# An expert's chunks past the third, moved from the end of the stage into the third chunk's condition

## The chip, the cores and the metric

The kernel runs on one core of a Trainium2 chip. Five engines work at once, each through its own list of instructions: TensorE (PE in the profile, PEld for its weight loads), VectorE (DVE), ScalarE (ACT), GpSimd (POOL) and SyncE (SP, which only starts transfers here). Rows with a small q behind the engine (PEldq, POOLq) are what its sequencer does: branches, semaphores, transfers that it issues. The metric is the device time of one launch in microseconds (us), lower is better.

## What is computed

Three parts in a row, on 1152 tokens of 512 numbers; the second and third matter here. Cut to what counts (`lg` are the logits of a token over eight experts):

```python
x = attention(q, k, v)                       # (1152, 512)
# part 2: each token goes to its best expert; an expert takes the first `capacity` of its tokens
e = argmax(x @ w_gate);  p = softmax value of e
out[i] = p[i] * (relu(x[i] @ w1[e]) @ w2[e]) if kept else 0        # capacity is 288
# part 3: tokens with x @ w_skip > 0 go through experts of their own, without a capacity
x[i] += p[i] * (relu(x[i] @ v1[e]) @ v2[e])
```

So how many tokens an expert gets is known only when the kernel runs: up to 288 in part 2, and in part 3 up to 1152.

## The kernel before

**Staging.** Attention ends at about 350 us. Then `experts(m, ...)` runs twice, for part 2 (m = 0, about 350 to 510 us) and for part 3 (m = 1, about 560 us to the end), with the routing of part 3 between them. The rows of an expert's tokens lie together in a scratch tensor `xs` in device memory, and an expert's rows are worked on in chunks of 128. Weights are loaded once per expert (`raw`), split into a high and a low part by ACT and DVE (`hi`, `lo`), while PE works on the expert before.

**One expert.** The first chunk of every expert is computed without a condition (`block_t`, whose matmuls are at L937, L947 and L957). Then comes a condition for the second chunk (L1172, more than 128 tokens), in it a choice between a whole and a half chunk (L1173), and in it the condition for the third chunk (L1178, more than 256) with its own choice (L1179). The tokens of chunk 2 and 3 are read from `xs` by `load_x` (L901). An expert's result goes to the output by an indirect transfer that POOL issues in `put` (L885).

**What is past the third chunk.** NPRE is 3, so three chunks are 384 tokens. For an expert with more, `rest` (from L1105) runs a loop, one more chunk for each turn. It stands at the end of the stage: a condition at L1188 on the largest of the eight counts (computed with the counts, L324), and in it, for each of the eight experts, a loop of at most one turn that loads and splits its weights again (`reload`) and calls `rest`.

**What follows a stage.** Behind m = 0, five loads by SP (L1215) read the output back for part 3. They wait for all the puts. PE goes on at once with the first chunk of the eighth expert (`last_block`), into which the transposes `gx` (L258) of the rows read back are mixed. Behind m = 1 the kernel ends.

**Conditions.** Each engine has its own copy of each condition: it reads the count, compares and branches. All code of a condition's body lies in the engine's list between the branch and the join. An engine that doesn't enter runs a short block in its place that brings the semaphores to the values which the body would have left; PE's block first waits for PE's own semaphore, that is until its matmuls so far are done. Rows of the trace with EVENT_SEMAPHORE or INC_SWDGE_SEM at a condition's line are that block, so they are there only where it was not entered. The order of the code is the order of the program, there is no scheduler.

Of the kernel before, what the change touches and what calls it, by code (L numbers as in the profile page):

```python
# [8 lines left out]
F32 = mybir.dt.float32  # L9
F32R = mybir.dt.float32r  # L10
BF16 = mybir.dt.bfloat16
I32 = mybir.dt.int32
AF = mybir.ActivationFunctionType
ALU = mybir.AluOpType
AX = mybir.AxisListType

P = 128
# [4 lines left out]
def fused_kernel(  # L22
# [15 lines left out]
    nc = tc.nc  # L38
    B, H, S, D = q.shape
    SQ = S // 2  # L40
    N, DM = out.shape
    E = wg1.shape[1]
    F = w1a.shape[2]
    KD = DM // P
    KF = F // P
# [6 lines left out]
    ROW = DM + 8  # L52
    REG = N
    NPRE = 3
# [4 lines left out]
    keep = ctx.enter_context(tc.tile_pool(name="keep", bufs=1))  # L59
# [86 lines left out]

    slot_i = keep.tile([P, NT], I32, name="slot_i")
    cnt = [keep.tile([P, E], F32, name=f"cnt{m}") for m in range(2)]
    cnt_i = [keep.tile([1, E + 1], I32, name=f"cnt_i{m}") for m in range(2)]
    mask = [keep.tile([P, E, NPRE], F32, name=f"mask{m}") for m in range(2)]  # L150

    def masks(m):
# [160 lines left out]
    def count(ps_r, ohs, limit, m):  # L313

        t = ps_r()[:, 0:E]
        mms = [o[:, j, :] for o, n_o in ohs for j in range(n_o)]
        for n, o in enumerate(mms):
            nc.tensor.matmul(t, ones, o, start=(n == 0), stop=(n == len(mms) - 1))
        if limit is not None:
            nc.vector.tensor_scalar(cnt[m], t, limit, None, op0=ALU.min)  # L320
        else:
            nc.vector.tensor_copy(cnt[m], t)
        nc.vector.tensor_copy(cnt_i[m][:, 0:E], cnt[m][0:1, :])
        nc.vector.tensor_reduce(out=cnt_i[m][:, E : E + 1], in_=cnt_i[m][:, 0:E], axis=AX.X, op=ALU.max)  # L324

    def warm(ps, n):

# [68 lines left out]
    with ExitStack() as actx:  # L396
# [328 lines left out]
        def flush(x, n):  # L725
            for _ in range(min(n, len(x))):
                x.pop(0)()

        ex = []
        for idx in range(len(items) + LAG):  # L730
# [6 lines left out]
            if cur and at in (0, NFC):  # L737
                flush(preps, len(preps))
                m = cur[0] + 1 + (at > 0)
# [14 lines left out]
            if cur:  # L754
                n, c = cur
                if at in (NFC - 1, 2 * NFC):
                    flush(preps, len(preps))
                m = n + (2 if at < NFC else 3)
# [9 lines left out]
            if old:  # L768
                n, c = old
# [16 lines left out]
        wp = [wctx.enter_context(tc.tile_pool(name="wp0", bufs=2, **kw))]  # L786
        w_t = {}
# [63 lines left out]
    with ExitStack() as mctx:  # L851
# [67 lines left out]
        def new_xx(name):  # L919
            return xo.tile([P, 2, KD, P], F32R, tag="xx", name=name)  # L920
# [165 lines left out]
                )  # L1086
            put(m, yt, dropped, x, HP)

        def reload(m, e):

            for half in range(2):
                hi, lo = w_t[m, e, half] = tuple(
                    wp[0].tile([P, KD * F], F32R, tag=t, name=f"{t}r{m}_{e}_{half}") for t in ("hi", "lo")
                )
                kk = (KD, KF)[half]
                src = ((w1a, w2a), (w1b, w2b))[m][half][e].rearrange("(c p) f -> p c f", p=P)
                for r in range(4):
                    raw = hp.tile([P, F], F32, tag="hs", name="raw")
                    c = slice(r * kk // 4, (r + 1) * kk // 4)
                    s = slice(r * F, (r + 1) * F)  # L1100
                    nc.sync.dma_start(out=raw.rearrange("p (c f) -> p c f", c=kk // 4), in_=src[:, c, :])
                    nc.scalar.copy(hi[:, s], raw)
                    nc.vector.tensor_tensor(out=lo[:, s], in0=raw, in1=hi[:, s].bitcast(F32), op=ALU.subtract)

        def rest(m, e, n_e, xx):  # L1105

            iv = sm.tile([P, 1], F32, tag="iv", name="iv")
            nc.vector.tensor_scalar_add(iv, rowid[:, 0:1], float(NPRE * P))

            pad = sm.tile([P, 1], F32, tag="pad", name="pad")  # L1110
            nc.vector.tensor_tensor(out=pad, in0=cnt[m][:, e : e + 1], in1=rowid[:, 0:1], op=ALU.add)
            big = sm.tile([P, 1], F32, tag="big", name="big")
            nc.vector.tensor_scalar(big, pad, float(REG), BIG, op0=ALU.is_ge, op1=ALU.mult)
            pi = sm.tile([P, 1], I32, tag="pi", name="pi")
            nc.vector.scalar_tensor_tensor(out=pi, in0=pad, scalar=float(e * REG), in1=big, op0=ALU.add, op1=ALU.add)
            z = xb.tile([P, ROW], F32, tag="x2", name="z", bufs=1)
            nc.vector.memset(z, 0.0)
            nc.gpsimd.indirect_dma_start(
                out=xs,
                out_offset=bass.IndirectOffsetOnAxis(ap=pi, axis=0),  # L1120
                in_=z,
                in_offset=None,
                bounds_check=E * REG - 1,
                oob_is_err=False,
            )
            with tc.For_i(NPRE * P, n_e, P) as i:
                lt = sm.tile([P, 1], F32, tag="lt", name="lt")
                nc.vector.tensor_tensor(out=lt, in0=cnt[m][:, e : e + 1], in1=iv, op=ALU.is_le)
                x = xb.tile([P, ROW], F32, tag="x2", name="xr", bufs=1)
                nc.sync.dma_start(out=x, in_=xs[bass.ds(i + e * REG, P), :])  # L1130
                xprep(x, xx)
                block_t(m, e, x, xx, lt, [], [], c_tile, d_tile)
                nc.vector.tensor_scalar_add(iv, iv, float(P))

        def experts(m, first, count_all, loads=()):


            x, xx = load_x(m, 0, 0), new_xx("xx0")
            two_parts(first, xx)
            count_all()  # L1140
            masks(m)
            x_n = load_x(m, 1, 0)
            x_1 = load_x(m, 0, 1)
            flush(loads, len(loads))
            for e in range(E):
                late = []
                steps = split_ops(m, e + 1, late) if e + 1 < E else []
                preps = []
                x_nn = load_x(m, e + 2, 0) if e + 2 < E else None
                none = [mask[m][:, e, c : c + 1] for c in range(NPRE)]  # L1150
                if e + 1 < E:
                    x_1n = load_x(m, e + 1, 1)
                if m == 0 and e == E - 1:
                    xx_1, xx = xx, new_xx("xx0")
                    xprep(x, xx)
                else:
                    if m == 0 and e == E - 2:
                        xx_1, xx_n = new_xx("xx1"), new_xx("xxn")
                        preps += [lambda: xprep(x_1, xx_1), lambda: xprep(x_1n, xx_n)]
                    else:  # L1160
                        if e + 1 < E:
                            xx_n = new_xx("xxn")
                            preps.append(lambda: xprep(x_n, xx_n))
                        xx_1 = new_xx("xx1")
                        preps.append(lambda: xprep(x_1, xx_1))
                    block_t(m, e, x, xx, none[0], steps, preps, a_tile, b_tile)
                if e == 0:
                    _, vals = nc.values_load_multi_w_load_instructions(cnt_i[m][0:1, :], min_val=0, max_val=N)
                n_e = vals[e]
                x_2 = xb.tile([P, ROW], F32, tag="x2", name=f"x{m}_{e}_2", bufs=1)  # L1170
                xx_2 = new_xx("xx2")
                with tc.If(n_e > P):  # L1172
                    with tc.If(n_e > P + HP) as more:  # L1173
                        load_x(m, e, 2, x_2)
                        block_t(m, e, x_1, xx_1, none[1], [], [lambda: xprep(x_2, xx_2)], c_tile, d_tile)
                    with more.Else():
                        block_h(m, e, x_1, xx_1, none[1], [], [], c_tile, d_tile)
                    with tc.If(n_e > 2 * P):  # L1178
                        with tc.If(n_e > 2 * P + HP) as more:  # L1179
                            block_t(m, e, x_2, xx_2, none[2], [], [], d_tile, c_tile)  # L1180
                        with more.Else():
                            block_h(m, e, x_2, xx_2, none[2], [], [], d_tile, c_tile)
                flush(late, len(late))
                if e + 1 < E:
                    x, xx, x_1, x_n = x_n, xx_n, x_1n, x_nn
            kept = [w_t[m, E - 1, half] for half in range(2)]

            with tc.If(vals[E] > NPRE * P):  # L1188
                xxr = new_xx("xxr")
                for e in range(E):  # L1190
                    with tc.For_i(NPRE * P, vals[e], N):
                        reload(m, e)
                        rest(m, e, vals[e], xxr)
            w_t[m, E - 1, 0], w_t[m, E - 1, 1] = kept
            return x, lambda fill, yt: block_t(m, E - 1, x, xx, none[0], fill, [], a_tile, b_tile, yt)

        x_last, last_block = experts(0, first, lambda: count(lambda: b_tile([P, 512], "pc0"), ohs, cap[:, 0:1], 0))
# [15 lines left out]
        for c, n in ((0, 1), (1, 2), (3, 2), (5, 2), (7, 2)):  # L1213
            src = out[c * P : (c + n) * P, :].rearrange("(c p) d -> p c d", p=P)
# [123 lines left out]
```

## Time and profile before

| | us |
|---|---|
| median of three runs | 720.62 (719.03 to 723.29) |
| the profiled execution, its own time | 716.99 |
| its span, from the first instruction to the last | 715.1 |

| engine | busy us | share of the span |
|---|---|---|
| PE | 660.8 | 92% |
| PEld | 487.7 | 68% |
| DVE | 446.7 | 62% |
| ACT | 436.1 | 61% |
| POOL | 128.4 | 18% |

PE is busy nearly all the time, so time is lost where PE stands still: each gap on PE is read with what ended it. The granted TensorE clock has a mean of 0.982 of full speed over the execution. An engine's instructions reach it by transfers of their own, the queues q8 (PE) and q14 (the others).

### The profile page before, as it was taken

What the parts mean: (1) busy time and instruction counts of PE and PEld (TensorE: products, weight loads), DVE (VectorE), ACT (ScalarE), POOL (GpSimd) and SP (SyncE); (2) the same over time, 40 slices, a digit from 0 to 9 for tenths busy, and PEclk for the clock granted to TensorE, in tenths of its full rate; (3) what the DMA queues carried; (4) which work ended last, traced back from release to release, by engine and by line L of the source; (5) the groups of instructions that cost most, each with busy time, mean ns of one, the idle gap of its engine ahead of it and who ended that gap; (6) DMA issues with size and microseconds to landing.
All of it is one profiled execution on the core that took longest, in us unless ns stands there. A gap on an engine that the chain in (4) does not pass through costs nothing. (4 is left out here: it accounts for less than half of the span.)

```text
span 715.1 us, 11137 instructions
## 1 busy us (share of the span) xinstructions
PE 660.8 (92%) x3978; PEld 487.7 (68%) x3978; DVE 446.7 (62%) x822; ACT 436.1 (61%) x961; POOL 128.4 (18%) x147
## 2 busy tenths in 40 slices
PE   7899999999999999998888999999779889999994
PEld 6766666666776666655766867776558677777773
DVE  5755656665655755556698638942176788998221
ACT  5876767676756757672687638832170768886210
POOL 4322222222221331002201011010035110001010
PEclk9999999999999999999999999999997999999998
DMA  6142624050200314014799917960444798994000
GB/s 175 41 142 107 218 107 171 17 188 31 82 17 2 114 38 152 1 19 176 263 334 339 337 46 266 329 222 18 147 137 156 247 348 314 369 339 149 27 30 13
DMA packets 55598, 111.38 MB, mean 156 GB/s; under 512 B 5470, under 2 KB 14686, under 8 KB 55488
## 3 DMA queue, kind: packets, MB, share of 16 engines
q1 hardware_dynamic: 52128, 102.27, 41.6%
q0 software_dynamic: 3360, 7.72, 2.8%
q8 instruction: 59, 0.97, 0.6%
q14 instruction: 51, 0.42, 0.2%
HBM read 93.51 MB, written 19.71 MB: 158 GB/s over the span
## 5 line engine op out<-in xcount | busy, mean ns | idle before, releaser
L807 DVE TENSOR_TENSOR lo<-raw,hi 128x512 fp32r<-128x512 f32 x248 | 155.6, 684 | 6.3 <-ACT hi L817 3.8
L817 ACT CAST hi<-raw 128x512 fp32r<-128x512 f32 x256 | 143.0, 623 | 8.4 <-PEq L1172 4.0
L527 PE MATMUL s_ps<-kop,qop 128*128 128x384 f32 x480 | 125.2, 369 | 2.2 <-ACT a L571 1.9
L601 PE MATMUL pt<-ident,a 128*128 128x128 f32 x648 | 109.7, 283 | 3.3 <-ACT kop L476 1.1
L555 DVE TENSOR_REDUCE m<-s_ps 128x1 f32<-128x1152 f32 x72 | 97.6, 1356 | 24.2 <-PE s_ps L527 21.5
L571 ACT ACTIVATE a<-s_ps,m 128x384 f32<-128x384 f32 (+1 forms) x144 | 106.8, 747 | 3.3 <-DVE m L555 3.2
L476 ACT COPY at<-pt 128x384 f32<-128x384 f32 x144 | 68.2, 481 | 64.1 <-PE pt L601 64.0
L601 PEld LDWEIGHTS pt<-ident,a 128*128 128x128 f32 x648 | 71.5, 140 | 46.1 <-ACT at L476 13.0
L627 PE MATMUL pv<-at,vr 128*64 128x320 f32 (+1 forms) x576 | 97.9, 428 | 0.0
L476 DVE COPY at<-pt 128x384 f32<-128x384 f32 x72 | 39.8, 552 | 76.3 <-PE pt L601 74.1
L527 PEld LDWEIGHTS s_ps<-kop,qop 128*128 128x128 f32 x480 | 74.6, 186 | 5.9 <-ACT a L571 4.3
L885 POOL DMA_INDIRECT out_dram<-yt,ix x23 | 24.9, 1084 | 285.7 <-DVEq L1172 149.1
L937 PE MATMUL ph<-hi,xxn 128*128 128x512 f32 x224 | 61.5, 406 | 13.2 <-PEq L1172 8.0
L950 DVE TENSOR_TENSOR hl<-pg,hh 128x512 fp32r<-128x512 f32 x42 | 29.0, 689 | 67.5 <-ACT hh L949 67.3
L941 ACT ACTIVATE hs<-ph 128x512 f32<-128x512 f32 x42 | 25.1, 598 | 60.3 <-PE ph L937 40.2
L937 PEld LDWEIGHTS ph<-hi,xxn 128*128 128x128 f32 x224 | 41.8, 192 | 26.9 <-ACTq L1172 7.0
L957 PE MATMUL py<-lo,hh 128*128 128x512 f32 x168 | 52.5, 414 | 0.0
L957 PE MATMUL py<-hi,hh 128*128 128x512 f32 x168 | 46.7, 399 | 1.3 <-ACT hh L949 0.8
L466 POOL TENSOR_TENSOR qhl<-qr,qhl 96x384 fp32r<-96x384 f32 x30 | 29.9, 1014 | 95.7 <-DVE qhl L464 95.7
L627 PEld LDWEIGHTS pv<-at,vr 128*64 128x64 f32 x576 | 30.0, 135 | 23.8 <-issue 18.3
L957 PE MATMUL py<-hi,hl 128*128 128x512 f32 x168 | 46.0, 395 | 0.0
L949 ACT CAST hh<-pg 128x512 fp32r<-128x512 f32 x42 | 24.6, 587 | 29.6 <-PE pg L947 27.7
(170 smaller groups left out, 891.8 us busy)
## 6 DMA issues: line engine op xcount, KB each, us to landing
raw<-in_moe_w_dram SPq DMA_DIRECT2D x64, 1024.0 KB, 7.3
x<-xs SPq DMA_DIRECT2D x36, 260.0 KB, 6.4
xs<-xtok SPq DMA_DIRECT2D x8, 780.0 KB, 7.4
qr<-in_q_dram SPq DMA_DIRECT2D x16, 288.0 KB, 3.4
vr<-in_v_dram SPq DMA_DIRECT2D x8, 576.0 KB, 6.1
kr_None<-in_k_dram SPq DMA_DIRECT2D x7, 576.0 KB, 5.0
out_dram<-xtok SPq DMA_DIRECT2D x3, 768.0 KB, 7.7
x<-out_dram SPq DMA_DIRECT2D x4, 512.0 KB, 5.7
```

Source lines behind the costliest of these rows:

```text
L466: sub.tensor_tensor(out=t[:, 1, :, r, :], in0=qs, in1=t[:, 0, :, r, :].bitcast(F32), op=ALU.subtract)
L476: (nc.vector.tensor_copy if on_vector else nc.scalar.copy)(dst, src)
L527: i = nc.tensor.matmul(s_ps[0:M, bank[j], 0 : 3 * P], qop[n + r][:, part, o : o + M], kop[n + r][:, j, :], start=(part == 0 and r == (c == ...
L555: i = nc.vector.tensor_reduce(out=nm, in_=s_ps[:, lo : lo + 3, 0 : 3 * P], axis=AX.XY, op=ALU.max, negate=True)
L571: i = nc.scalar.activation(a[:, a0 : a0 + nb, :], s_ps[:, b0 : b0 + nb, 0 : 3 * P], AF.Exp, bias=nm, accum_out=t[:, c, n % 2, k : k + 1],)
L601: nc.tensor.transpose(ps[:, x * P : (x + 1) * P], a[:, g, x * P : (x + 1) * P], ident)
L627: nc.tensor.matmul(hold["pv"][j * D : (j + 1) * D, 0:w], vrt[i][:, j, c * D : (c + 1) * D], at_t[2 * i + j, part][:, c, :], start=(c == 0) ...
L807: eng.tensor_tensor(out=lo, in0=raw, in1=hi.bitcast(F32), op=ALU.subtract)
L817: nc.scalar.copy(hi, raw)
L937: lambda d=d, i=i, a=a, b=b: nc.tensor.matmul(ps, xx[:, a, d, :], w1[b][:, d, s], start=(d + i == 0), stop=(d == KD - 1 and i == 2))
L950: nc.vector.tensor_tensor(out=hl[:, fs, :], in0=ps, in1=hh[:, fs, :].bitcast(F32), op=ALU.subtract)
L957: lambda f=f, i=i, a=a, b=b: nc.tensor.matmul(py, a[:, f, :], w2[b][:, f, :], start=(f + i == 0), stop=(f == KF - 1 and i == 2))
```

## The change

`rest` is called with its expert: in the third chunk's condition, behind the third chunk, there is one more condition, for more than 384 tokens, and `rest` in it, which takes the weights that are still there. The condition at the end of the stage goes away, with the reloading, the eight loops and the maximum of the counts. `rest` uses the tiles of the third chunk, `x_2` and `xx_2`, for the zero rows and the rows of a turn. Lines of the changed kernel: L1172 is L1153 there, L1178 is L1159, L937 is L936, L957 is L956, L1215 is L1189, and the new condition is L1164, with `rest`'s loop at L1108.

```diff
-    cnt_i = [keep.tile([1, E + 1], I32, name=f"cnt_i{m}") for m in range(2)]
+    cnt_i = [keep.tile([1, E], I32, name=f"cnt_i{m}") for m in range(2)]
...
-        nc.vector.tensor_copy(cnt_i[m][:, 0:E], cnt[m][0:1, :])
-        nc.vector.tensor_reduce(out=cnt_i[m][:, E : E + 1], in_=cnt_i[m][:, 0:E], axis=AX.X, op=ALU.max)
+        nc.vector.tensor_copy(cnt_i[m], cnt[m][0:1, :])
...
-        def reload(m, e):
...
-        def rest(m, e, n_e, xx):
+        def rest(m, e, n_e, x, xx):
...
-            z = xb.tile([P, ROW], F32, tag="x2", name="z", bufs=1)
-            nc.vector.memset(z, 0.0)
+            nc.vector.memset(x, 0.0)
...
             with tc.For_i(NPRE * P, n_e, P) as i:
...
-                x = xb.tile([P, ROW], F32, tag="x2", name="xr", bufs=1)
                 nc.sync.dma_start(out=x, in_=xs[bass.ds(i + e * REG, P), :])
...
                             block_h(m, e, x_2, xx_2, none[2], [], [], d_tile, c_tile)
+                        with tc.If(n_e > NPRE * P):
+                            rest(m, e, n_e, x_2, xx_2)
                 flush(late, len(late))
...
-            kept = [w_t[m, E - 1, half] for half in range(2)]
-
-            with tc.If(vals[E] > NPRE * P):
-                xxr = new_xx("xxr")
-                for e in range(E):
-                    with tc.For_i(NPRE * P, vals[e], N):
-                        reload(m, e)
-                        rest(m, e, vals[e], xxr)
-            w_t[m, E - 1, 0], w_t[m, E - 1, 1] = kept
```

The order of the instructions changes in the same way for each of the sixteen experts. On PE before, at the end of the first expert, the last matmuls of the half third chunk, the joins of the conditions (the unconditional branches; where one waits for PE, that is the block for not entering), and the second expert's first chunk:

```order
L1012 MATMUL py<-hi_0_1_3537,hx 128x512 x3
L1012 MATMUL py<-lo_0_1_3538,hx 64x512 x4
L1179 UNCONDITIONAL_BRANCH
L1178 UNCONDITIONAL_BRANCH [waits PE_49]
L1172 UNCONDITIONAL_BRANCH [waits PE_49]
L937 MATMUL ph<-hi_1_0_3845,xxn 128x512 [waits Activation_49]
L937 MATMUL ph<-hi_1_0_3845,xxn 128x512 x3
```

The same place on PE in the changed kernel, up to the first matmuls of `rest`:

```order
L1011 MATMUL py<-hi_0_1_3537,hx 128x512 x3
L1011 MATMUL py<-lo_0_1_3538,hx 64x512 x4
L1160 UNCONDITIONAL_BRANCH
L1164 COMPARE_AND_BRANCH
L1108 COMPARE_AND_BRANCH
L1108 UNCONDITIONAL_BRANCH [waits PE_49]
L1108 UNCONDITIONAL_BRANCH [waits barrier_Pool_Activation_PE_DVE_SP_release]
L1307 BRANCH_PREFETCH_HINT
L911 MATMUL psx<-ident,x_0_2_4058 128x128 [waits DMAHW1_49]
L911 MATMUL psx<-ident,x_0_2_4058 128x128 x3
```

All of `rest` now stands between the third chunk and the joins, in 35 rows of PE for each expert (a matmul row counts its matmuls, and each matmul has a weight load): 147 instructions. A branch over the second chunk (L1172, which has the third chunk and `rest` in it) passes 423 instructions of PE before and 573 now, one over the third chunk 207 and 357. At the end of the stage m = 0, PE before:

```order
L1179 UNCONDITIONAL_BRANCH
L1178 UNCONDITIONAL_BRANCH [waits PE_49]
L1172 UNCONDITIONAL_BRANCH [waits PE_49]
L1188 COMPARE_AND_BRANCH
L1191 COMPARE_AND_BRANCH
L1191 UNCONDITIONAL_BRANCH [waits PE_49]
L1191 UNCONDITIONAL_BRANCH [waits barrier_Pool_Activation_PE_DVE_SP_release]
```

And now, where the rows from L936 on are the first chunk of the eighth expert, which the next part of the program begins with:

```order
L1164 UNCONDITIONAL_BRANCH [waits PE_49]
L1159 UNCONDITIONAL_BRANCH [waits PE_49]
L1153 UNCONDITIONAL_BRANCH [waits PE_49]
L936 MATMUL ph<-hi_7_0_7317,xx_7881 128x512 [waits Activation_49]
L936 MATMUL ph<-hi_7_0_7317,xx_7881 128x512 x3
```

Behind the last join there is no branch at L1188 and none of the some 300 rows of its body any more. On POOL at the same place before (DMASW0 to 7 are the eight semaphores that the puts use in turn):

```order
L1188 ISA [waits DMASW4_49,DMASW5_49,DMASW3_49,DMASW6_49,DMASW2_49,DMASW7_49,DMASW1_49,DMASW0_49]
L1188 UNCONDITIONAL_BRANCH
L1210 MEMSET x_0_8718 128x5x8 [waits DVE_49,PE_49,Activation_49]
L1211 COPY x_0_8718<-tokrow 128x5 [waits Pool_49]
L1210 MEMSET x_1_8719 128x5x8 [waits DVE_49,PE_49,Activation_49]
```

And on POOL now:

```order
L1164 ISA [waits DMASW4_49,DMASW3_49]
L1164 UNCONDITIONAL_BRANCH
L1159 ISA [waits DMASW4_49,DMASW3_49,DMASW2_49]
L1159 UNCONDITIONAL_BRANCH
L1153 ISA [waits DMASW3_49,DMASW4_49,DMASW2_49,DMASW1_49]
L1153 UNCONDITIONAL_BRANCH
L1184 MEMSET x_0_8314 128x5x8 [waits PE_49,Activation_49]
```

POOL's block for not entering waited for all eight at the end of a stage, and now waits for those of two puts at the new condition, in the third chunk of each expert.

## Rows read from the trace of the kernel before

**Rows 1.** The page: busy us of each engine (share of the span) and its instructions.

```profile
PE 660.8 (92%) x3978; PEld 487.7 (68%) x3978; DVE 446.7 (62%) x822; ACT 436.1 (61%) x961; POOL 128.4 (18%) x147
```

**Rows 2.** Line L1188, whole span: count, duration min/median/max in ns, first and last start.

```profile
L1188 PEldq COMPARE_BRANCH  x2: 4003/4468/4932, 504.6 to 702.7; - x2
L1188 POOLq COMPARE_BRANCH  x2: 50/50/50, 506.2 to 706.2; - x2
```

**Rows 3.** Timeline of PE, 503 to 524: start, duration, instruction, [idle before <- releaser].

```profile
503.07 1.10 PE L957 MATMUL py<-hi,hl 128*128 128x512 f32 x4
508.77 2.04 PE L937 MATMUL ph<-hi,xx 128*128 128x512 f32 x4 [4.61 <-PEq L1188]
...
516.27 0.60 PE L258 MATMUL gx<-ident,x 128*128 128x128 f32 x4
```

**Rows 4.** Windows: length, busy us (count) of PE, PEld, DVE, ACT, POOL, granted clock, DMA.

```profile
508.37:511.78 3.41, 3.01 (x7) 2.46 (x8) 0.00 (x0) 0.00 (x0) 0.70 (x5) 0.50 0.12 19
...
391.10:394.50 3.40, 3.40 (x17) 2.81 (x18) 2.76 (x6) 2.44 (x5) 0.32 (x1) 1.00 1.04 330
...
586.88:590.30 3.42, 3.42 (x10) 2.64 (x9) 2.95 (x6) 1.10 (x3) 0.98 (x1) 0.50 1.06 383
```

**Rows 5.** Chain of work that ended last, 490 to 530: start, duration, what.

```profile
510.59 0.35 SPq L1215
```

**Rows 6.** Line L1188 again, 504 to 513; then L258, 500 to 530.

```profile
L1188 POOLq EVENT_SEMAPHORE  x4: 17/43/43, 509.4 to 509.6; - x4
...
L1188 POOLq INC_SWDGE_SEM  x1: 612/612/612, 509.7 to 509.7; - x1
...
L258 PEldq EVENT_SEMAPHORE  x5: 51/51/51, 514.0 to 527.9; - x5
```

**Rows 7.** The end: POOL's last put (timeline), then L1188 and L1333, from 690 on.

```profile
706.25 0.98 POOL L885 DMA_INDIRECT out_dram<-yt,ix  x1 [11.48 <-DVE ix L882]
...
L1188 POOLq EVENT_SEMAPHORE  x4: 17/43/201, 709.0 to 709.4; - x4
...
L1188 POOLq INC_SWDGE_SEM  x1: 1052/1052/1052, 709.5 to 709.5; - x1
...
L1333 POOLq DRAIN  x3: 46/107/3662, 710.5 to 714.8; - x3
```

**Rows 8.** Line L1178, whole span; one row of the timeline; L1178 from 499 to 504.

```profile
L1178 PEldq EVENT_SEMAPHORE  x2: 51/51/51, 504.2 to 666.6; - x2
...
666.97 1.20 PE L937 MATMUL ph<-hi,xxn 128*128 128x512 f32 x4 [0.44 <-PEq L1178]
...
L1178 PEldq COMPARE_BRANCH  x1: 622/622/622, 501.2 to 501.2; - x1
```

**Rows 9.** Line L1172, whole span; a row of the waits (total us, times, longest).

```profile
L1172 PEldq COMPARE_BRANCH  x16: 70/3446/5440, 354.9 to 676.5; - x16
L1172 PEldq EVENT_SEMAPHORE  x11: 51/51/51, 358.7 to 641.0; - x11
...
PE ph L937 <- PEq L1172: 8.0, 6, 1.9
```

**Rows 10.** L1178 from 664 to 668; L1172 from 630 to 641.

```profile
L1178 PEldq COMPARE_BRANCH  x2: 190/262/333, 664.4 to 666.7; - x2
...
L1172 PEldq COMPARE_BRANCH  x1: 1051/1051/1051, 637.3 to 637.3; - x1
```

**Rows 11.** Timeline of PE around three skipped second chunks.

```profile
391.03 1.67 PE L937 MATMUL ph<-hi,xxn 128*128 128x512 f32 x6 [1.74 <-issue]
...
585.60 1.17 PE L937 MATMUL ph<-hi,xxn 128*128 128x512 f32 x4 [1.93 <-PEq L1172]
...
643.35 0.40 PE L937 MATMUL ph<-hi,xxn 128*128 128x512 f32 x1 [1.27 <-issue]
```

**Rows 12.** 100 to 300, attention: windows; PE's instruction queue (packets, MB, share).

```profile
100.00:300.00 200.00, 197.14 (x1393) 135.88 (x1392) 121.06 (x207) 138.63 (x349) 44.88 (x50) 1.00 0.23 78
...
q8 instruction: 11, 0.18, 0.4%
```

More of the change, by code (lines that the diff above doesn't have):

```diff
@@ L1087, in block_h @@
             put(m, yt, dropped, x, HP)
-        def reload(m, e):
[L1091 to L1103, printed above, removed]
-        def rest(m, e, n_e, xx):
+        def rest(m, e, n_e, x, xx):
             iv = sm.tile([P, 1], F32, tag="iv", name="iv")
@@ L1120, in rest @@
                 out_offset=bass.IndirectOffsetOnAxis(ap=pi, axis=0),
-                in_=z,
+                in_=x,
                 in_offset=None,
```

## The prediction

> **What bounds the kernel now.** I read the page first: PE is busy for 92% of the span [rows 1], so a change pays where it takes away time in which PE stands still, or where PE has nothing left to do. Next come the lines of the conditions. The block for not entering tells how the data falls: the second chunk was left out by eleven of the sixteen experts [rows 9], the third by two of the five others [rows 8], and the condition at L1188 both times [rows 6, 7]. So three third chunks ran and not one chunk past the third. The loops, the reloading and `rest` never run, before or after. What the change moves is code that all engines jump over, and a jump is not free: PE's branch at L1188 took 4.00 us the first time and 4.93 the second [rows 2], where one that goes on in order takes 0.07 (the minimum) [rows 9]. A skipped second chunk cost PE's sequencer 3.4 us in the median [rows 9]. Most of that is not seen, since PE is still working on matmuls issued before: of all those branches only 8.0 us are idle time before a matmul, six gaps of at most 1.9 us [rows 9]. The forecast is thus a balance of jumps: two long ones less, and sixteen experts whose skipped code is 147 instructions longer.
>
> What a jump costs can be read too. PE's instructions come in packets: 11 between 100 and 300 us, while PE ran 1393 matmuls and 1392 weight loads [rows 12], so some 253, with the few semaphore rows 256, to a packet of 16 KB. Straight code shows no gap at a packet. A skip over 423 instructions passes 1.65 packets, and its 3.4 us say that the packet it lands in isn't there yet.
>
> [...]
>
> **The change part by part.** The base is the profiled execution, 716.99 us, of which 715.1 are its span; the median of three is 720.62, and a sum of gains and losses is put on the median.
>
> *A. The end of the first stage.* Now PE ends its matmuls at 504.17 (503.07 and 1.10) [rows 3], branches at 504.60 for 4.00 us [rows 2], and starts again at 508.77, a gap of 4.61. [...] After the change there is no branch here, but the one over the eighth expert's third chunk (at 501.2, 0.62 us now [rows 8]) passes 357 instructions instead of 207, by my layout of the code over a packet's border. I charge it the median of a skip, 3.4 us, up to 4.0: it ends at 504.6 to 505.2, under PE's last matmuls or just behind. With the drain that the joins keep (0.44 [rows 8]) PE would go on at about 505.2, 3.6 us earlier. But by the layout it lands four instructions ahead of a border, and a second stop of 1.5 us (between 1.27 and 1.74 [rows 11], see D) makes it 506.7, 2.1 earlier. [...] What is late next are the five loads of the output. They are issued at 510.59, held by POOL [rows 5], whose branch at 506.2 takes until 509.4 and whose catch-up of the put semaphores ends at 510.3 [rows 2, 6]. Without this stall they go out 2.4 to 3.1 us earlier. PE had the first of them at 514.0 [rows 6], before the first transposes at 516.27 [rows 3]: some 2 us of slack. They allow 2.4 plus that slack, 4.4. Bounds -2.1 and -5.3; I take **-3.6**, close to 2.1 and 1.7, for a PE that stops twice and keeps its clock. VectorE, ScalarE and SyncE lose a branch of the same kind here, off this path.
>
> *F. The end of the kernel.* PE's second branch at L1188 lies behind its last work. POOL decides: its last put is issued by 707.23, the branch stalls it until 709.0, semaphores and catch-up last until 710.51, then a drain of 3.66 ends the kernel [rows 7]. Now POOL skips 39 instructions there, with the same kind of catch-up before the drain: 707.2 and 1.05 make 708.3 instead of 710.5, -2.2, and a little less to catch up. If the drain waits for the put to land, which no row separates, nearly nothing is won: -0.3 to -3.3; I take **-2.4**.
>
> *B. A join more in an entered third chunk.* Experts 3 and 6 of the first stage skip `rest` by a branch over 147 instructions, by the layout at most into the packet behind, so without a fetch, but the block behind it waits until PE's matmuls are done. The nearest row is the same wait at a skipped third chunk, 0.44 us [rows 8]. Two of them **+0.8**, 0.4 to 1.3. The third such expert is the last, where PE has nothing behind it.
>
> *C. The third chunk that expert 6 of the second stage leaves out.* Its branch took 0.33 us at 664.4 [rows 10], with 0.44 idle behind it [rows 8]. Over 357 instructions it leaves its packet 20 instructions after entering it. I charge 3.4 us less what PE has queued: it worked until 666.53, 2.1 us after the branch. That makes 667.8 and a semaphore, where it now goes on at 666.97: **+1.1**; 0 if the next packet is there, 2.9 for a skip like the longest, 5.44 [rows 9].
>
> *D. Where a skip lands.* Behind two of the eleven skips PE stood still a second time, 1.74 and 1.27 us, not by a semaphore [rows 11]: there the skip lands within the last tenth of a packet, and the next one isn't there yet. I laid both programs out in packets of 256; the layout of before puts exactly these two in that place. With 147 more for each expert there are four, besides the one in A. Two more at 1.5: **+3.0**, from 0 (a border missed by a few instructions) to 3.5.
>
> *E. The shortest skip* took 1.05 us [rows 10], since it crossed one border only, long after the packet before was entered; over 573 instructions all eleven cross two or three. At most the longest gap of a skip, 1.93 [rows 11]; I take **+0.7**, the mean of the gaps over all eleven (8.0/11).
>
> *The clock.* A gap of 1.93 us was followed by a half clock for 3.42 us [rows 4, 11], costing 1.7. C or D may bring one such gap: **+0.9**, 0 to 3.4.
>
> *The rest.* The maximum of eight counts and its value, -0.1. SP's loads of the next expert's rows get a wait on POOL's catch-up; they are issued a whole expert ahead of their use, so nothing; were that lead gone, it would cost the length of such a catch-up, 0.6 to 1.05 [rows 6, 7].
>
> Sum: -3.6 - 2.4 + 0.8 + 1.1 + 3.0 + 0.7 + 0.9 - 0.1 = +0.4. So 717.4 for an execution like the profiled one, 721.0 on the median.
>
> **The rivals.** *Faster: the longer skips stay covered.* PE hides four fifths of its skips now (8.0 of eleven times 3.4); if a second packet passed costs no more than the first, and landings near a border are no worse than before, C, D, E and the clock vanish, and A loses its second stop, up to the -4.4 that the loads allow: -4.4 - 2.4 + 0.8 - 0.1 = -6.1, 714.5. For it: the five skips of eleven that show no gap at all [rows 9]. Against it: the two second stops that only the place of the code explains [rows 11].
>
> *Slower: every skip now loses the packets at hand.* PE arrives after each skip with nothing prefetched behind the landing, and runs dry again. With six second stops instead of two, 4 x 1.5 = 6.0 in place of 3.0, and two half clocks, 3.4 in place of 0.9, the sum is +5.9, 726.5. It decides from about four new second stops. For it: 1.27 and 1.74 are there already; against it: nine skips of eleven have none now. What the two longest branches took, 4.0 and 4.9 [rows 2], is within what skips of 423 instructions took [rows 9], so no row shows yet that a longer way costs more.
>
> [...]
>
> *It doesn't do what it says.* The reloading that it saves is never run with these counts, so that part is nothing in every case above, and no rival of its own.
>
> **How the numbers follow.** Forecast, within some 3 us of its time, 0.53; the faster rival 0.25; the slower 0.22. A measurement of this kernel can tell about 0.5%, 3.6 us, from no change. The range reaches to the faster rival's time and to the slower one's, leaving some of each out: 714.5 to 726.5. Faster by over 0.5% is the faster rival, less the part of it that falls short of 3.6 and with what of the forecast goes beyond: 0.25. Slower in the same way: 0.22. Within: 0.53.
>
> **What would show it.** Right: a PE gap near 504 of 1.0 to 2.6 us in place of 4.61, and no half clock there; the output's loads issued near 508; the span ending some 2 us closer behind the last put; a new gap of 1 to 2 us behind the third chunk of expert 6; four or five stops named "issue" behind skips. Wrong: skip times at L1153 much over 3.4 us in the median, more half clocks than before, or a drain that grows by what POOL gained. If neither end of a stage gains, A and F were read wrongly, and the change is only a loss.

## The result, and the profile after

The changed kernel takes 724.31 us (721.01 to 729.08), the kernel before 719.83 over the same measurement: a ratio of 1.0108, with an interval of 1.0063 to 1.0152. It is slower by 1.1%, where "about the same" was forecast; the time itself lies inside the range. A second measurement (e9 below) gave 1.0117. The profiled execution took 721.01 us, its span is 719.2, 4.1 more than before.

PE's work is what it was [rows 1]:

```profile
span 719.2 us, 11150 instructions
...
PE 661.7 (92%) x3978; PEld 488.1 (68%) x3978; DVE 446.0 (62%) x820; ACT 436.3 (61%) x961; POOL 134.7 (19%) x147
```

The end of the first stage gained what step A hoped for, and a little more. The timeline of PE there (start, duration, instruction, idle time before it and what ended it), to be held against [rows 3]:

```profile
511.86 1.20 PE L936 MATMUL ph<-hi,xx 128*128 128x512 f32 x4 [0.43 <-PEq L1159]
519.10 0.63 PE L258 MATMUL gx<-ident,x 128*128 128x128 f32 x4 [0.94 <-DMA x<-out_dram]
```

The gap of 4.61 us is 0.43, and from PE's restart to the first `gx` it is 7.2 us instead of 7.5 although PE now waits for the loads at its end. From PE's last matmul of the stage (511.43) to `gx` there are 7.7 us where there were 12.1: 4.4 us gained.

The end of the kernel gained too. POOL's last put, then the rows of the new condition and of the end of the program, from 700 on, as [rows 7]:

```profile
713.33 0.98 POOL L884 DMA_INDIRECT out_dram<-yt,ix  x1 [11.46 <-DVEq L1164]
...
L1164 POOLq INC_SWDGE_SEM  x1: 1045/1045/1045, 713.5 to 713.5; - x1
...
L1307 POOLq DRAIN  x3: 46/107/3657, 714.7 to 719.0; - x3
```

From the put to the drain there are 1.4 us where there were 4.3, and the drain is as long as before: 2.9 gained. So 7.3 us were won at the two ends, and still the span is 4.1 longer: 11.4 us net were lost elsewhere. The waits of the whole span (total us, times, longest) and the branch over the second chunk show where not to look:

```profile
PE ph L936 <- issue: 8.6, 4, 3.3
PE ph L936 <- PEq L1153: 7.6, 9, 2.0
...
L1153 PEldq COMPARE_BRANCH  x16: 70/3736/5497, 354.9 to 683.6; - x16
```

The gaps that a skip itself leaves are 7.6 us, before 8.0 [rows 9], and the median branch is 3.7 us for 3.4 (both over all sixteen branches, of which five went on in order; of the eleven skips alone it is 3.9 for 3.7): passing 573 instructions costs hardly more than passing 423. What grew is the first row: four stops that no semaphore explains, 8.6 us, where before had two of 1.74 and 1.27 [rows 11]. The timeline shows all four, two of them with the matmuls from the landing on:

```profile
377.01 1.20 PE L936 MATMUL ph<-hi,xxn 128*128 128x512 f32 x4 [0.76 <-issue]
...
452.76 1.17 PE L936 MATMUL ph<-hi,xxn 128*128 128x512 f32 x4 [1.50 <-PEq L1153]
453.77 1.09 PE L936 MATMUL ph<-lo,xxn 128*128 128x512 f32 x4
454.70 2.02 PE L936 MATMUL ph<-hi,xxn 128*128 128x512 f32 x8
460.02 1.22 PE L936 MATMUL ph<-lo,xxn 128*128 128x512 f32 x2 [3.29 <-issue]
...
572.76 1.17 PE L936 MATMUL ph<-hi,xxn 128*128 128x512 f32 x4 [2.00 <-PEq L1153]
573.77 0.63 PE L936 MATMUL ph<-lo,xxn 128*128 128x512 f32 x2
577.19 0.73 PE L936 MATMUL ph<-lo,xxn 128*128 128x512 f32 x2 [2.78 <-issue]
...
635.85 0.50 PE L936 MATMUL ph<-hi,xxn 128*128 128x512 f32 x1 [1.75 <-issue]
```

PE skips, lands, runs some matmuls and stands still again. Step D had counted four such skips from its layout, without naming them; the trace has them 12, 16, 6 and 10 matmuls behind the landing. With the weight loads that is 24, 32, 12 and 20 instructions, so at least the second lies outside the last tenth of a packet (26 instructions) that D looked at.

The trace also holds the packets of PE's queue q8 themselves. Behind the four landings the next packet sets out only 1.6, 4.8, 2.1 and 2.0 us after the first matmul, is moved in 0.9 to 1.1 us, and PE goes on 1.2 to 1.4 us after that. For the stop at 460.02 no packet of q8 moves between 453.0 and 457.4; from 457.4 to 459.9 there is one (its row there: packets, MB, share of the DMA engines):

```profile
q8 instruction: 1, 0.02, 2.7%
```

The granted clock (the column before the last two) falls to 0.50 of full speed behind two of the four stops:

```profile
459.81:463.22 3.41, 3.20 (x10) 2.62 (x11) 0.43 (x1) 1.05 (x2) 0.00 (x0) 0.50 1.05 415
637.30:640.71 3.41, 3.41 (x11) 2.73 (x11) 1.42 (x3) 2.09 (x4) 0.00 (x0) 0.50 1.00 334
497.35:500.76 3.41, 3.41 (x10) 2.64 (x9) 0.69 (x1) 0.27 (x1) 0.00 (x0) 0.50 0.29 85
```

and behind a third gap that step B had undersized, at the join behind expert 6 of the first stage, where PE waits for VectorE's new join and not only for itself (1.04 us of idle time stood at this place before); the last row is the third chunk of step C:

```profile
496.32 0.63 PE L911 MATMUL psx<-ident,x 128*128 128x128 f32 x4 [2.12 <-DVEq L1164]
...
674.11 1.20 PE L936 MATMUL ph<-hi,xxn 128*128 128x512 f32 x4 [1.65 <-PEq L1159]
```

### The profile page after: what moved, and what is told of

Same layout as the page of the kernel before. It is cut to its first block, busy times and chain, and to the rows that moved or that the text cites. A ratio compares the mean times of both kernels' runs of the same rounds, so it can differ in the third digit from the quotient of the medians.

```text
span 719.2 us, 11150 instructions
## 1 busy us (share of the span) xinstructions
PE 661.7 (92%) x3978; PEld 488.1 (68%) x3978; DVE 446.0 (62%) x820; ACT 436.3 (61%) x961; POOL 134.7 (19%) x147
## 5 line engine op out<-in xcount | busy, mean ns | idle before, releaser
L884 POOL DMA_INDIRECT out_dram<-yt,ix x23 | 27.9, 1212 | 294.2 <-DVEq L1153 153.6
L936 PE MATMUL ph<-hi,xxn 128*128 128x512 f32 x224 | 62.1, 408 | 12.5 <-PEq L1153 7.6
L936 PEld LDWEIGHTS ph<-hi,xxn 128*128 128x128 f32 x224 | 42.1, 193 | 28.0 <-issue 9.1
L956 PE MATMUL py<-lo,hh 128*128 128x512 f32 x168 | 52.3, 413 | 0.0
L956 PE MATMUL py<-hi,hh 128*128 128x512 f32 x168 | 47.5, 405 | 0.6
L956 PE MATMUL py<-hi,hl 128*128 128x512 f32 x168 | 46.4, 398 | 0.0
```

The costliest lines, as they stand in the source:

```text
L884: i = nc.gpsimd.indirect_dma_start(out=out, out_offset=bass.IndirectOffsetOnAxis(ap=ix[:M], axis=0), in_=yt[:M], in_offset=None, bounds_ch ...
L936: lambda d=d, i=i, a=a, b=b: nc.tensor.matmul(ps, xx[:, a, d, :], w1[b][:, d, s], start=(d + i == 0), stop=(d == KD - 1 and i == 2))
L956: lambda f=f, i=i, a=a, b=b: nc.tensor.matmul(py, a[:, f, :], w2[b][:, f, :], start=(f + i == 0), stop=(f == KF - 1 and i == 2))
```

## The experiments

The theory after the result: it matters **where in a packet a skip lands**, not how far it goes; the packet behind the landing sets out only after the landing (1.6 to 4.8 us after the first matmul there, at the four stops above). The rivals: the **length** of the skips; the new **conditions and joins**. Each kernel is compared with the kernel before, timed on the same chip: one chip for e1 to e4, a second for e5 to e8, a third for e9 and e10. Across chips the ratios are compared.

| kernel | skip, PE instructions, about | us | ratio (95% interval) |
|---|---|---|---|
| changed, again (e9) | 573 | 726.34 | 1.0117 (1.0065 to 1.0168) |
| e1, 24 more in `rest` | 621 | 715.84 | 0.9944 (0.9907 to 0.9981) |
| e2, 29 more | 631 | 723.66 | 1.0044 (1.0013 to 1.0075) |
| e8, 30 more | 633 | 710.08 | 0.9877 (0.9828 to 0.9927) |
| e10, 33 more | 640 | 714.69 | 0.9937 (0.9906 to 0.9969) |
| e5, short body | 436 | 706.80 | 0.9817 (0.9768 to 0.9866) |
| e3, no condition at the end | 423 | 706.78 | 0.9799 (0.9754 to 0.9845) |
| e6, end for one expert | 423 | 710.63 | 0.9854 (0.9787 to 0.9920) |
| e7, end of stage 1 only | 423 | 719.97 | 0.9966 (0.9919 to 1.0012) |
| e4, old and new condition | 573 | 730.72 | 1.0137 (1.0071 to 1.0202) |

**Moving the landings with code that never runs (e1, e2, e8, e10, beside e9).** In the loop of `rest`, which no expert enters:

```diff
             with tc.For_i(NPRE * P, n_e, P) as i:
...
                 nc.sync.dma_start(out=x, in_=xs[bass.ds(i + e * REG, P), :])
+                pp = x_tile([P, KD, P], "pp")
+                for k in range(24):   # 29 in e2, 30 in e8, 33 in e10
+                    nc.tensor.transpose(pp[:, k % KD, :], x[:, k % KD * P : (k % KD + 1) * P], ident)
                 xprep(x, xx)
```

> The changed kernel with 24 more transposes in the loop of `rest`, which is never entered: what runs is the same, but each skip on PE is 48 instructions longer (621 instead of 573), and by the layout in packets of 256 no skip lands in the last third of a packet (of the changed kernel four of eleven do: behind them PE stood still 0.76, 3.29, 2.78 and 1.75 us, and twice with a half clock behind it). Theory, the place of landing costs: the four stops go (-8.6) and two half clocks (-3.4), so 9 to 12 us faster than the changed kernel, 2 to 6 faster than before. Rival, the length of a skip costs: the same as the changed kernel or slower, 4 to 8 us over before. Rival, the new joins in the third chunks cost: the same as the changed kernel.

> The same with 29 more transposes instead of 24: skips 10 instructions longer than with 24 (631). By the layout none lands near a packet's end in the first stage, but four in the second stage 5 to 13 instructions ahead of one, and two right at a border. Theory, place: at those four PE runs dry for 2.8 to 3.8 us each, 13 in sum, with up to four half clocks (up to 6.8) behind: 10 to 20 us slower than with 24. Rival, length: within 1 us of the kernel with 24, since the skip is 2% longer. Rival, joins: the same as with 24.

> The changed kernel with 30 more transposes in the never-entered loop of `rest`, one more than e2: each skip two instructions longer (634 for 632). In the second stage all six landings move from just ahead of a packet's border to just behind one. Theory, place: the five stops of e2 (12.9 us) and its half clocks behind them go: 8 to 15 us faster than e2, 712 to 716, as the kernel with 24 or faster, since the third chunk left out by expert 6 now also lands one border on, without a fetch. Rival, the length alone: the same as e2, 723.7.

> The changed kernel once more, on the same chip as e10. Theory, place: four skips land ahead of a packet's border, 722 to 728, 0.5 to 1.3% over before.

> The changed kernel with 33 more transposes in the never-entered loop, the longest skips of all (640 instructions of PE). By the layout every skip lands in the first half of a packet; the third chunk left out by expert 6 of the second stage crosses two borders again, as with 24. Theory, place: no second stop, 711 to 717, faster than before and at least 7 faster than e9; between e8 and e1 by the 1.2 us of that third chunk and its clock. Rival, length: slower than e9, over 725.

With 24 more transposes, and longer skips, the kernel is 1.6% faster than the changed one by the ratios, some 12 us, and a little faster than before. With 29 it is 8 us slower than with 24, and one transpose more, 30, makes it 1.7% faster again, some 12 us by the ratios, where the code that runs has not changed by an instruction. Length falls as the reason for the loss: the kernel with the longest skips (e10) is over 11 us faster than the changed kernel (e9), and its median branch takes the same time, 3.7 us. The gaps that the skips themselves leave have no order by length either: 9.2 us in e9, 9.6 in e1, 8.3 in e2, 11.9 in e8 and 9.0 in e10. The branch over the second chunk in e9, e8 and e10 (their lines are L1153, L1156, L1156):

```profile
L1153 PEldq COMPARE_BRANCH  x16: 70/3672/5833, 354.2 to 683.9; - x16
```

```profile
L1156 PEldq COMPARE_BRANCH  x16: 70/4057/5631, 354.4 to 670.6; - x16
```

```profile
L1156 PEldq COMPARE_BRANCH  x16: 70/3732/4936, 354.3 to 676.9; - x16
```

The stop shows itself best in e2 and e8 at the same skip, that of the second stage's second expert, on PE's timeline. In e2 PE lands, issues one matmul and stands for 5.31 us; the next expert the same:

```profile
582.75 1.09 PE L956 MATMUL py<-hi,hl 128*128 128x512 f32 x4
584.89 0.47 PE L936 MATMUL ph<-hi,xxn 128*128 128x512 f32 x1 [1.06 <-PEq L1156]
590.68 1.65 PE L936 MATMUL ph<-hi,xxn 128*128 128x512 f32 x3 [5.31 <-issue]
...
606.05 1.17 PE L936 MATMUL ph<-hi,xxn 128*128 128x512 f32 x4 [0.30 <-PEq L1156]
610.00 1.87 PE L936 MATMUL ph<-lo,xxn 128*128 128x512 f32 x4 [2.78 <-issue]
```

In e8 the same skip leaves the same gap, and then PE runs on:

```profile
576.88 1.09 PE L956 MATMUL py<-hi,hl 128*128 128x512 f32 x4
579.02 1.17 PE L936 MATMUL ph<-hi,xxn 128*128 128x512 f32 x4 [1.05 <-PEq L1156]
580.03 1.09 PE L936 MATMUL ph<-lo,xxn 128*128 128x512 f32 x4
580.96 2.03 PE L936 MATMUL ph<-hi,xxn 128*128 128x512 f32 x8
```

Over the whole span the waits named "issue" ahead of `ph` are 10.6 us in e2 and 0.6 in e8, e2 first:

```profile
PE ph L936 <- issue: 10.6, 4, 5.3
```

```profile
PE ph L936 <- issue: 0.6, 2, 0.4
```

e9 is the changed kernel again, and it tells how steady a stop is. Its four stops are behind the same skips and have nearly the same sum, but singly they are 2.71, 0.36, 2.05 and 3.19 us, where the first trace had 0.76, 3.29, 2.78 and 1.75:

```profile
PE ph L936 <- issue: 8.3, 4, 3.2
```

Not all expectations held. e2 is 7.8 us slower than e1, short of the 10 to 20 expected: its trace has five stops behind skips, of 1.2 to 5.3 us, 12.9 in sum, but its profiled execution, at 729.89 us, lies well over its median of 723.66. In e1 the stops went, but not the half clocks: behind gaps of 1.82 to 2.62 us there are four stretches of 3.41 us in its trace. In e10 one stop of 1.95 us remained, at the end of the first stage, where the layout had none. And e8 has a ratio 0.6% under those of e1 and e10, but the intervals overlap, so that this is not settled. Its trace has 0.44 us of idle time at the third chunk of the second stage's expert 6 where e1 has 1.82, as the layout had it; its clock of 0.991 over the span is that of its fastest execution, the others have 0.979 to 0.985.

**Conditions and joins without the length (e5).** The body of the new condition is cut to 11 instructions of PE:

```diff
                         with tc.If(n_e > NPRE * P):
-                            rest(m, e, n_e, x_2, xx_2)
+                            nc.vector.memset(x_2, 0.0)
+                            pp = x_tile([P, KD, P], "pp")
+                            for k in range(5):
+                                nc.tensor.transpose(pp[:, k % KD, :], x_2[:, k % KD * P : (k % KD + 1) * P], ident)
```

> The changed kernel with the body of its new condition cut to a memset of the tile and five transposes (11 instructions of PE instead of 147): chunks past the third are not computed (no expert has one here). The new conditions and joins stay, the skips are as short as before (436 instead of 573), and by the layout no skip lands in the last tenth of a packet. Theory, place and length: within 3 us of the kernel without any condition at the end (e3, 706.8), that is 10 to 13 faster than before, and the joins cost at most those 3. Rival, the joins cost: over 5 us more than e3, near the padded kernel e1 (715.8).

It is as fast as the kernel with no condition at all past the third chunk (e3), with intervals of half a percent to either side: the sixteen conditions and their joins cost a few us at most. Its layout had no landing in the last tenth, but two in the last fifth (at 0.84 and 0.81 of a packet), and these two stopped PE, 19 and 23 matmuls behind the landing, which shows that the tenth of step D was too narrow. Its waits:

```profile
PE pg L946 <- issue: 2.2, 1, 2.2
PE ph L936 <- issue: 1.9, 1, 1.9
```

One thing stays open here. e1 and e10, with no stop and with one, are still 1.2 to 1.5% behind e3 and e5. Some of it is in the traces: against e3, e1 has 1.82 us for 0.43 at the third chunk of the second stage's expert 6, 9.6 for 6.3 in the gaps of the skips, and more half clocks. Whether a long body costs a few us besides the place of its landings is shown by no run.

**The ends (e3, e6, e7).** e3 leaves out the block from `kept` to the last line with `kept`; e7 puts the condition under `if m == 0`; e6 has only the first expert in it:

```diff
             with tc.If(vals[E] > NPRE * P):
                 xxr = new_xx("xxr")
-                for e in range(E):
+                for e in range(1):
                     with tc.For_i(NPRE * P, vals[e], N):
```

> The kernel before without the condition at the end of each stage, and nothing in its place: chunks past the third are not computed by it (no expert has one here). Theory: both ends gain what the changed kernel's trace shows, 4.4 us between the stages (PE's stall behind its last matmuls, and the half clock) and 3.0 at the end of the kernel, and the code of the second stage moves to places where no skip lands near a packet's end, 1.3 more: 7 to 9 us faster than before. Rival, the ends gave nothing (the loads of the output or the final drain take their place): within 2 us of before.

> The kernel before with its condition at the end of each stage cut to the first expert's loop instead of eight, so the branch there passes 174 instructions of PE instead of 1378: other experts' chunks past the third are not computed (none has one here). The landings of the second stage move with it, again with one near a packet's end. Theory, the stall at the end is the fetch of code far away: it goes, 4 to 7 us between the stages with the half clock and 3 at the end, 7 to 10 faster than before. Rival, the condition itself costs (its joins, the catch-up of all eight put semaphores): within 3 us of before.

> The kernel before without the condition at the end of the second stage (no chunk past the third there), with that of the first kept. All that PE does stays where it is. Theory: the last drain starts without POOL's stall, 3.0 us faster than before, nothing else. Rival, the drain takes up the stall: within 1 us of before.

Without the ends the kernel is 2.0% faster, 13.7 us, more than the ends themselves can give: the profiled executions differ by 10.0 us (715.1 and 705.0), of which 5.6 are there at PE's first matmul behind the end of the first stage, the stop of 1.74 at 389 included, 6.7 at the last matmul, and 3.3 come behind it. The rest is between the profiled execution of before, at 716.99 us, and its median of 720.48 on this chip. e6 shows that the condition is not at fault but the eight copies of its body: over 174 instructions the branch that took 4.0 and 4.9 us takes 0.23 and 0.36:

```profile
L1188 PEldq COMPARE_BRANCH  x2: 228/296/364, 504.5 to 698.7; - x2
...
PE ph L937 <- PEq L1188: 0.8, 1, 0.8
```

For e7 the interval reaches over no change, so the time alone doesn't decide. In its trace the drain starts beside the put instead of 3.3 us behind its end, and takes 4.7 us instead of 3.7; from the end of the put to the end of the span there are 4.5 us for 7.8, so the 3.0 that were expected at this end are in the trace:

```profile
705.33 0.98 POOL L885 DMA_INDIRECT out_dram<-yt,ix  x1 [11.48 <-DVE ix L882]
...
L1334 POOLq DRAIN  x3: 46/117/4727, 705.3 to 710.6; - x3
```

**The losses alone (e4).** The kernel before with `rest` of the changed kernel, under its condition in the third chunk, and the old end kept:

```diff
                             block_h(m, e, x_2, xx_2, none[2], [], [], d_tile, c_tile)
+                        with tc.If(n_e > NPRE * P):
+                            rest_in(m, e, n_e, x_2, xx_2)
```

> The kernel before with the changed kernel's condition in each third chunk added, and its own condition at the end of the stage kept: the losses of the change alone. Theory: in the first stage the landings are the changed kernel's (stops of 0.8 and 3.3 instead of 1.7, one half clock, 1.7), in the second only one lies near the last tenth of a packet; the joins cost 1.1 behind expert 6 of the first stage and 0.4 behind expert 3, the left-out third chunk of expert 6 in the second stage 1.2: 4 to 8 us slower than before. Rival, the losses come from elsewhere (joins of all experts): over 10 slower. Rival, they are only noise: within 2 us of before.

It is slower by 9.9 us, above what was expected. Its trace has stops of 1.33, 2.83 and 1.56 us, and besides longer gaps behind the skips themselves, up to 3.8:

```profile
PE ph L937 <- PEq L1200: 13.3, 8, 3.8
...
PE ph L937 <- issue: 4.2, 2, 2.8
```

Two skips left 3.75 and 3.85 us there, and none left that much in the changed kernel with skips of the same length. The packets show that the one PE lands in came late: ahead of 363.39 it set out 4.0 us behind the branch, and ahead of 583.39 another packet was moved first. Why is open. The gains of e3 and the losses of e4 don't add up to the change either (-14 and +10 against +5 to +8). Each of the three kernels lays its second stage out differently, since taking the old end away moves all of it by 1378 instructions; that this is the reason was not tried.

## Why the prediction was wrong

- *What bounds, and that nothing of `rest` runs*: right. PE runs the same 3978 matmuls; the difference is in jumps over code that is not entered and in what follows from them. One reading is off: the median of 3.4 us for a skip [rows 9] is over all sixteen branches, and of the eleven skips alone it is 3.7.
- *A*, -3.6: 4.4 in the trace, but the size was met by luck. The path was not that of a PE that stops twice: the branch over the eighth expert's third chunk took 1.02 us and not 3.4, and the second stop that was charged for the landing four instructions ahead of a border did not come (gap 0.43; a packet moved from 510.21 to 511.32, while PE still worked). What held PE in the end was the loads, which the part had named as a bound: they went out 4.8 us behind PE's last matmul instead of 6.4, and the first `gx` waited 0.94 us for them. The bound of -5.3, 3.6 and 1.7, counts the half clock behind the gap: before, the clock stood at 0.50 for 3.41 us there [rows 4], half of which is 1.7; in the changed kernel it stayed at 1.00 (511.43 to 514.90).
- *F*, -2.4: 2.9. The drain did not wait longer for the put (3.66 us in both).
- *B*, +0.8: 0.44 behind expert 3, as charged, but 2.12 for 1.04 behind expert 6, since there the next work of PE is a transpose that waits for VectorE's join; and a half clock behind it. Kernels e1, e2, e5, e8 and e10 show 0.53 to 0.55 at this place, so the size hangs on the rest of the layout as well, and not on the join alone.
- *C*, +1.1: 1.65 for 0.44, so +1.2.
- *E*, +0.7: the gaps of the skips went from 8.0 to 7.6; nothing.
- *D*, +3.0: **this is the step that failed**, by its size. It counted four stops, and four came. But they became 8.6 us, 5.6 more than the two of before, and not 3.0. I had given each stop the mean length of the two that were in the trace, 1.5. A stop is no constant: at these four it is, within some 0.3 us, the time until the next packet's first matmul, less the time that PE takes to reach the border. From the first matmul behind the landing to the first one of the next packet it is 3.8, 7.3, 4.4 and 4.3 us in the changed kernel and 4.3 and 2.2 before. A matmul with its weight load, two instructions, is issued every 0.23 us at full clock (four from 453.77 to 454.70 above), so PE has worked off the 12, 16, 6 and 10 matmuls in front of the border after 2.8, 3.7, 1.4 and 2.3 us. That leaves 1.0, 3.6, 3.0 and 2.0 us, where the stops measured 0.76, 3.29, 2.78 and 1.75. Read in this way, the two times of before [rows 11] would have widened the bounds, to some 6 us for the four stops at 4.3 each and under 1 at 2.2, but they would not have given the 8.6. The time to the next packet is not a constant of a kernel either: in e9 it is 5.8, 5.9, 3.7 and 5.8 us at the same four skips.
- *The clock*, +0.9: mis-sized as well, and by as much as D. Three half clocks among the experts are new (behind the 3.29, the 1.75 and the 2.12, 1.7 us each), one of before is gone: +3.4. More half clocks than before was one of the signs that the prediction had named for being wrong. They don't follow the length of a gap alone: there is none behind the 2.78.

So the sum would have been -4.4 - 2.9 + 1.5 + 1.2 + 5.6 + 3.4 = +4.4, close to the +4.1 of the span, while the prediction had +0.4: D and the clock were 5.1 too low together, the other terms 1.1 too high. What stands in no term nearly cancels: a fourth new half clock, at 354.0 ahead of the first skip, costs 1.5 and longer waits in the routing between the stages 2.0, and a shorter half clock there (6.8 us for 10.2), shorter gaps of the skips and the matmuls behind `gx` give as much back. The slower rival had the sign, and its terms, 6.0 for stops and 3.4 for the clock, are near the measured 5.6 and 3.4; but it had them from six stops of 1.5 in all, where four of 2.1 on average came. Of the faster rival the first half holds, that a longer way costs no more; what falls is that landings would be no worse.

The length of a skip hardly shows in its time. The eleven skips of a second chunk took 3.7 us in the median in the kernel before and 3.9 in the changed one; over all sixteen branches the medians of before, the changed kernel, e1, e2, e3, e8, e9 and e10 lie between 3.4 us (before, 423 instructions) and 4.1 (e8, 633), with 3.7 for the longest skips (e10, 640). Shorter branches took 0.2 to 0.6 us: 0.32 and 0.33 over 147 instructions (the new condition), 0.23 and 0.36 over 174 (e6), 0.33 and 0.62 over 207 [rows 8, 10]. In straight code, from 100 to 300 us of the kernel before, eleven packets came [rows 12] and no idle time of PE is put down to "issue"; behind a landing the way into the next packet cost up to 5.31 us (e2).

The best version that the experiments gave, of those that compute everything, is the changed kernel with 30 never-executed transposes (e8): 1.2% faster than the kernel before, and 2.4% faster than the changed kernel by the two ratios (0.9877/1.0117). It computes all that the changed kernel computes. The 706.8 of e3 and e5, which leave out chunks past the third, show what is left for one that keeps the code which is jumped over short.

## What to carry to other kernels

Code that never runs has a place, and its place has a price: the branch over 423 to 640 instructions held PE's sequencer for 3.4 to 4.1 us here (medians over all sixteen branches of a run; 3.4 over 423 instructions, 3.7 over 640), and behind some landings shortly ahead of a packet's end PE stood still again, for 0.36 to 5.31 us. When a change moves the length of a skipped body, lay the program out in packets (here 16 KB, some 253 matmuls and weight loads of PE [rows 12] and 3 semaphore rows), list the landings, and bound each stop by the time to the next packet less the matmuls up to the border; that time was 2.2 to 7.3 us in the two kernels and differed between two executions of one kernel, so a range is all that it gives. Two kernels that differ in dead code alone were 1.7% apart (e2 and e8). The fastest kernels had one copy of the body at the end (e6) or a short body (e5); neither computes all that the others do, so a whole kernel of this kind was not built.

## What the runs showed of the hardware

Two instructions more in each of sixteen bodies that are never entered changed the time by 1.7%, some 12 us (e2 and e8). The first matmul of the next packet came 3.8 to 7.3 us behind a landing in the changed kernel, while weights were being loaded (the share of the DMA engines from the four landings until the packet set out was 0.87 to 1.05). The move of a packet took 0.9 to 1.6 us there and 0.9 to 1.4 in attention, where that share was 0.23 (in the kernel before [rows 12]); what varied was when it set out, 1.6 to 4.8 us after the first matmul behind the landing. Whether the loads delay that was not tried. The kernel before spread from 714 to 731 us over its executions, e3 from 705.9 to 707.8; the cause of the difference is open.
